# Attention into soft-MoE on one core: V products, transposes and batch work of a pair in one block on TensorE

## The chip, the cores and the metric

The kernel runs on one NeuronCore of a Trainium2 chip. Five engines work side by side, each with its own instruction queue in program order: TensorE (PE, matmuls; its weight loads are listed apart as PEld), VectorE (DVE), ScalarE (ACT), GpSimd (POOL) and SyncE (SP, used here only to issue transfers). Matrix products land in PSUM, which DVE and ACT read; transfers (DMAs) run between the chip's DRAM and SBUF on sixteen DMA engines. The metric is the device time of one execution in microseconds (us).

## The reference

Attention over 8 batches, 12 heads, 448 tokens and a head width of 64, whose denominator has one term more than a softmax, followed by a soft mixture of experts over the 3584 x 768 result. Cut to what matters:

```python
scores = q @ k.T / sqrt(64)
m = max(scores, axis=-1)
e = exp(scores - m)
attn = e / (sum(e) + exp(-m) + 1e-9)
x = (attn @ v)  as [8*448, 12*64]

logits = x @ phi                     # [3584, 32]: 8 experts, 4 slots each
d = softmax(logits, axis=0)          # over all 3584 tokens
slot_in = d.T @ x                    # [32, 768]
h = relu(slot_in[e] @ w1[e])         # 768 -> 1024, per expert
slot_out = h @ w2[e]                 # 1024 -> 768
c = softmax(logits, axis=1)          # over the 32 slots
out = c @ slot_out                   # [3584, 768]
```

## The kernel before

Heads are taken two at a time: 48 pairs, six to a batch, three to a "group" `g` that is loaded together. The two heads of a pair stand on partitions 0 to 63 and 64 to 127. Their score matmuls have 64 rows each, and neighbours in the queue that use different halves run at the same time; the V products and turns use all 128 rows. The schedule is manual: each engine runs its instructions in the order in which the Python code emits them, and semaphores follow from the tiles.

The parts of one pair `n`:

- `T(n)` transposes q and k by 28 small matmuls into one PSUM tile (`ps_t`, L224) and copies it to SBUF, on ACT for the first six pairs and the first pair of each group, else on DVE (L227, L229).
- `A`, `A1`: score blocks with queries on the partitions, for the row maxima. A pair has seven: six of 128x448 (L268 and L246) and one in which the two heads share a tile (L256). Each has its reduction on DVE into `mx` (L270, L250, L259).
- `W1(g)`, `W2(g)`, `W3(g)`, once for three pairs: POOL negates the maxima (L277), PE turns them into rows (L297, L298), ACT copies these to `mT` and takes the exponentials of the negated maxima, `ec` (L303, L306, L309).
- `Bk`, `AB`: score blocks with keys on the partitions (L354, L332), less the maximum by a second matmul that adds a row of `mT` (L358, L335), then ACT's exp into a buffer `e2` or `e1` (L360, L338). `AB` also emits `A1` blocks of a later pair, one ahead of its own matmuls and one behind.
- `V(g)` arranges v for a group, with a column of ones, on POOL.
- `AV(n, i, qs)`: V products, 32 matmuls of 65 columns per pair into `ps_av` (L393); the column of ones gives the sum of the exponentials.
- `N1(n)` copies `ps_av` to `ubuf` (ACT; DVE for the last four pairs; L405). `N2(n)` adds 1e-9 and `ec` to the sums and takes the reciprocal (two small DVE operations, L414, L415), then multiplies into `x` (three operations, L419, L423, L424, on POOL, for the last four pairs on DVE).
- `PX(n)` transposes the pair's part of x by four matmuls and ACT copies 512 columns to `xT` (L445, L451).

`P(b)` holds the mixture's work for one batch, as six steps: logits (L471) with their copy and row maxima; the turned logits (L496); the maximum over tokens (L508); the exponentials; the slot sums (L539) with the fading of what has been added so far; the turn of the combine weights (L544) and their sums `crec`.

The loop runs over `s` = 0 to 47, each with two half steps `y`, numbered `hs = 2s + y`. From hs = 5 on, the first half step emits two `AB` of pair s, then the last two i of the V products of pair s-1 for the three full query blocks, and its eight products for the fourth, then `N1`. The second emits one `AB`, `Bk(s, 3)` with the shared maxima block in it, `T(s+6)`, every third time W2 and W3, the first two i of the V products of pair s itself (12 matmuls), a step of P if one is due (`post`), `PX(s-2)`, and `N2(s-1)`. The maxima run four pairs ahead, so that none are left from s = 44 on. Loads by POOL follow at the end of each s: q and k, v, then expert weights, cast from f32 to bf16 on the way (`half_at`, `part_at`, `col_at`, `narrow_at`).

Buffers set the order as much as the queues do: PSUM pool `psA` has three banks, used in turn by the maxima blocks, `ps_t` and all tiles of P; `psB` has four, for the exp blocks, W2 and PX; `psV` one, for `ps_av`. There are five `e2` buffers and one `e1`.

The weights fill SBUF: eleven tiles `W` (w1 of eight experts, w2 of the first three), the twelfth half and the rest of w2 in `R`, where q, k, x and the exponentials lie, as these come free. The second column half of w2 for experts 4 to 7 is cast ahead into DRAM (`wd`) and brought in by SP (`load_second`, L141) at the end of attention.

Behind the loop stand the last batch's P, the hidden layers (`hidden`, L748: experts 0 to 3, then 4 to 7), the slot products (`slots`, L764), and the output, 3584 rows by 768 in f32, whose transfers fill the last 25 us.

Of the kernel before, what the change touches and what calls it, by code (L numbers as in the profile page):

```python
# [24 lines left out]
HG = 6  # L25
# [6 lines left out]
def kernel(  # L32
# [38 lines left out]
    ident2 = const.tile([128, 128], BF16, name="ident2")  # L71
# [7 lines left out]
    NQK, NE, VPN, NATV = 7, 5, HG * 4 * VS, HG * 4 * D  # L79
    sizes = [("nq0", 2 * NP * S), ("nq1", 2 * NP * S), ("nv", NATV), ("qk6", 2 * S), ("wm1", 512),  # L80
             ("qk0", 2 * S), ("qk1", 2 * S), ("qk2", 2 * S), ("wm0", 512), ("qk3", 2 * S), ("vp0", VPN),
             ("qk4", 2 * S), ("x0", 4 * DD), ("qk5", 2 * S), ("e2", NE * 2 * S), ("e1", S), ("vp1", VPN),
             ("xT", KC * 512), ("x1", 4 * DD)]
# [8 lines left out]
    e1_t = part("e1", 0, S)  # L92
# [3 lines left out]
    xT = part("xT", 0, KC * 512).rearrange("p (j s) -> p j s", j=KC)  # L96
# [23 lines left out]
    W = keep.tile([128, 11 * KC * F], BF16, name="W")  # L120
    w_tile = lambda i: W[:, i * KC * F:(i + 1) * KC * F]
# [10 lines left out]

    dram = ctx.enter_context(tc.tile_pool(name="dram", bufs=1, space=bass.MemoryType.DRAM))
    wd = [dram.tile([128, E2, ND], BF16, name=f"wd{z}") for z in range(FK)]

# [7 lines left out]
    with ExitStack() as at:  # L143
# [8 lines left out]
        ubuf = pu.tile([128, 2, 7 * W65], F32, name="ubuf")  # L152
# [27 lines left out]
        for h in range(2):  # L180
            nc.vector.tensor_add(ident2[:, 64 * h:64 * h + 64], ident[:, 0:64], ident[:, 64:128])
# [22 lines left out]
        mx, ngm, ec, mT, eT, av, us = {}, {}, {}, {}, {}, {}, {}  # L204
# [32 lines left out]
        def A(n, i):  # L237
# [4 lines left out]
            if i < 3:  # L242
# [5 lines left out]
                for hl in range(2):  # L248
                    c = HG * i + 2 * pl + hl
                    nc.vector.reduce_max(mx[g][:, c:c + 1], pss[hl][:, 0:S], axis=AX.X)  # L250
            else:
# [6 lines left out]
                c = 3 * HG + pl  # L258
                nc.vector.reduce_max(mx[g][:, c:c + 1], ps[:, 0:S], axis=AX.X)  # L259

        def A1(n, i, hl):
# [7 lines left out]
            c = HG * i + 2 * pl + hl  # L269
# [3 lines left out]
        def W1(g):  # L273
# [4 lines left out]
            cols = lambda t: t[:, 0:3 * HG].rearrange("p (i c) -> p i c", i=3)[:, :, 2 * l0:2 * l1]  # L278
            o = w[:, 0:3, :].rearrange("p i (d c) -> p i d c", d=2)[:, :, :, 2 * l0:2 * l1]
            neg(o, cols(m).unsqueeze(2).to_broadcast([128, 3, 2, 2 * (l1 - l0)]))  # L280
            for hl in range(2):
                r = slice(64 - 64 * hl, 128 - 64 * hl)
                o = w[r, 3, :].rearrange("p (d c) -> p d c", d=2)[:, :, 2 * l0 + hl:2 * l1:2]
                neg(o, m[r, 3 * HG + l0:3 * HG + l1].unsqueeze(1).to_broadcast([64, 2, l1 - l0]))
            if l1 - l0 == NP:
                neg(nm, m)
            else:
                nc.gpsimd.memset(nm, 0.0)
                neg(cols(nm), cols(m))
                neg(nm[:, 3 * HG + l0:3 * HG + l1], m[:, 3 * HG + l0:3 * HG + l1])  # L290
            ngm[g] = nm

        def W2(g):
# [4 lines left out]
            nc.tensor.matmul(ps[:, 384:448], w[:, 3, :], ident2[:, 0:64], start=True, stop=True)  # L298
            st["ps_m"] = ps

        def W3(g):
# [3 lines left out]
            e = psm.tile([128, NP, 7], F32, tag="ec", name="ec", bufs=3)  # L305
            nc.scalar.activation(e[:, :, 0:6].rearrange("p l (i h) -> p i l h", i=3),  # L306
                                 ngm[g][:, 0:18].rearrange("p (i l h) -> p i l h", i=3, h=2),
                                 AF.Exp, scale=scale)
            nc.scalar.activation(e[:, :, 6], ngm[g][:, 18:21], AF.Exp, scale=scale)  # L309
            ec[g] = e  # L310


        def Bk(n, i, c=0):
# [11 lines left out]
            else:  # L325
# [3 lines left out]
                es = [e1_t]  # L329
# [69 lines left out]
        def N1(n):  # L399
# [4 lines left out]
            u = ubuf[:, n % 2, :].rearrange("p (s c) -> p s c", c=W65)  # L404
# [3 lines left out]
        def N2(n):  # L408
            g, pl = divmod(n, NP)
            b, pb = divmod(n, PB)  # L410
            u = us[n]
            eng = nc.gpsimd if on_pool(n) else nc.vector
            rec = psm.tile([128, 7], F32, tag="rec", name="rec", bufs=3)
            nc.vector.scalar_tensor_tensor(rec, u[:, :, D], 1e-9, ec[mg(n)][:, pl, :], op0=ALU.add, op1=ALU.add)  # L414
            nc.vector.reciprocal(rec, rec)  # L415
            x = xb[b % 2]
            c = pb * 128
            rec2 = psm.tile([128, 2], F32, tag="rec2", name="rec2", bufs=3)
            eng.tensor_mul(  # L419
                x[:, 0:3, c:c + 128].rearrange("p i (h d) -> p i h d", h=2),  # L420
                u[:, 0:6, 0:D].rearrange("p (i h) d -> p i h d", h=2),
                rec[:, 0:6].rearrange("p (i h) -> p i h", h=2).unsqueeze(3).to_broadcast([128, 3, 2, D]))
            eng.tensor_scalar(rec2, halfm, rec[:, 6:7], None, op0=ALU.mult)  # L423
            eng.tensor_mul(  # L424
                x[:, 3, c:c + 128].rearrange("p (h d) -> p h d", h=2),
                u[:, 6, 0:D].unsqueeze(1).to_broadcast([128, 2, D]),
                rec2.unsqueeze(2).to_broadcast([128, 2, D]))
# [10 lines left out]
        def PX(n):  # L438
# [4 lines left out]
            for i in range(4):  # L443
                o = (i % 2 if two else i) * 128
                nc.tensor.matmul(pss[i // 2 if two else 0][:, o:o + 128], x[:, i, c], ident if i < 3 else ident2,  # L445
                                 start=True, stop=True)
            if two:
                nc.scalar.copy(xT[:, pb, 0:256], pss[0][:, 0:256])
                nc.vector.tensor_copy(xT[:, pb, 256:512], pss[1][:, 0:256])
            else:  # L450
                nc.scalar.copy(xT[:, pb, :], pss[0])  # L451
# [183 lines left out]
        for s in range(NPAIR):  # L635
            for y in range(2):
# [16 lines left out]
                if hs < 5:  # L653
                    T(hs + 3)
# [232 lines left out]
```

## Time and profile before

| | |
|---|---|
| median of three runs | 310.31 us (310.02 to 310.5) |
| the profiled execution | 310.7 us, span 308.9 us |
| busy shares of the span | PE 89%, DVE 83%, ACT 81%, POOL 66% |
| attention in its steady form | 40.5 to 242.9 us, s = 3 to 43 |
| last four pairs without maxima | 242.9 to 260.4 us |
| last batch, experts | 260.4 to 282.9 us |
| output | to 308.9 us |

The profile is one execution. A line of groups or of the timeline gives the engine, the kernel's line, the operation, the tile written and the tile read with shapes, and the count; in the timeline the first two numbers are the start and the length in us, and a bracket at the end tells the idle time of the engine before it and who ended it. Lengths of neighbours on one engine overlap, so the pace is read from starts. A line of stretches has the stretch, its length, the busy time and count of PE, PEld, DVE, ACT and POOL, the granted TensorE clock, the DMA share and GB/s.

### The profile page before, as it was taken

How to read it: one execution, taken by the hardware profiler on the slowest of the kernel's cores; microseconds unless marked ns; L12 is line 12 of the kernel's file. 1: busy time of each engine (PE TensorE's matmuls, PEld its weight loads, DVE VectorE, ACT ScalarE, POOL GpSimd, SP SyncE). 2: the span in 40 equal slices, each digit the busy share in tenths (PEclk: the TensorE clock that was granted, in tenths of full speed). 3: DMA queues.
4: the chain of work that ended last, by engine and by line, in shares of the span. 5: the costliest groups of instructions: out<-in, count | busy, mean ns of one | idle time of the engine just before them, and what ended most of it. 6: DMA issues, size and time to landing. Idle time of an engine off the chain costs nothing.

```text
span 308.9 us, 12205 instructions
## 1 busy us (share of the span) xinstructions
PE 275.6 (89%) x5067; PEld 159.0 (51%) x5068; DVE 257.2 (83%) x607; ACT 249.3 (81%) x549; POOL 202.7 (66%) x403
## 2 busy tenths in 40 slices
PE   2899999999999999999999999999999899994810
PEld 1434456565666656665566566656665556451200
DVE  4778999999999999999999999999999566536930
ACT  2357599999999999999999999999999997236810
POOL 8682769788788878896889788879584863000000
PEclk9999999999999999999999999999999999999555
DMA  6999499999999999999999999999971999937997
GB/s 88 149 128 202 64 205 150 198 182 205 163 196 157 210 169 198 155 203 149 149 164 186 177 186 169 196 177 203 166 110 17 144 126 204 337 128 260 415 439 312
DMA packets 49350, 57.44 MB, mean 186 GB/s; under 512 B 2832, under 2 KB 41488, under 8 KB 48912
## 3 DMA queue, kind: packets, MB, share of 16 engines
q0 software_dynamic: 45536, 42.52, 90.1%
q1 hardware_dynamic: 3760, 14.16, 11.5%
q8 instruction: 39, 0.64, 0.8%
q14 instruction: 15, 0.12, 0.1%
HBM read 88.18 MB, written 14.16 MB: 331 GB/s over the span
## 4 chain that ended last, share of the span: by engine, by line
PE 50%; DVE 30%; ACT 7%; issue 4%; POOL 4%; DMA 1%; DVEq 0%; POOLq 0%
DVE mx L270 15%; PE ps_av L393 11%; PE ps_a L268 6%; PE ps_t L224 6%; PE ps_b L354 5%; PE ps_b L358 4%; DVE mx L250 3%; DVE mx L259 3%; PE ps_b L332 3%; PE ps_a L246 2%; DVE W L801 2%; DVE R L229 2%; PE ps_x L445 2%; ACT R L227 2%; PE ps_so L764 2%
## 5 line engine op out<-in xcount | busy, mean ns | idle before, releaser
L270 DVE TENSOR_REDUCE mx<-ps_a 128x1 f32<-128x448 f32 x248 | 136.6, 613 | 5.3 <-PE ps_a L268 5.1
L360 ACT ACTIVATE R<-ps_b 128x448 bf16<-128x448 f32 x272 | 131.0, 573 | 1.1 <-PE ps_b L358 0.8
L268 PE MATMUL ps_a<-R 64*128 64x448 bf16 x248 | 80.5, 352 | 1.8 <-DVE mx L270 1.8
L354 PE MATMUL ps_b<-R 64*128 64x448 bf16 x272 | 73.9, 353 | 0.9
L358 PE MATMUL ps_b<-mT,sel 64*128 64x448 bf16 x272 | 70.6, 350 | 0.0
L393 PEld LDWEIGHTS <-R 128*128 128x128 bf16 (+1 forms) x1536 | 50.5, 101 | 30.5 <-issue 26.4
L393 PE MATMUL ps_av<-R 128*128 128x65 bf16 (+1 forms) x1536 | 64.9, 196 | 0.1
L419 POOL TENSOR_TENSOR R<-ubuf,rec 128x384 bf16<-128x384 f32 x44 | 36.3, 825 | 37.9 <-DVE rec L415 23.4
L224 PEld LDWEIGHTS <-R 64*64 64x64 bf16 x1344 | 31.1, 113 | 19.2 <-issue 7.8
L338 ACT ACTIVATE R<-ps_b 128x448 bf16<-128x448 f32 x64 | 36.0, 579 | 5.9 <-PE ps_b L335 5.9
L224 PE MATMUL ps_t<-ident,R 64*64 64x64 bf16 x1344 | 32.0, 198 | 5.9 <-DMA R<-in_q_dram 4.3
L451 ACT CAST R<-ps_x 128x512 bf16<-128x512 f32 x47 | 28.1, 598 | 5.7 <-PE ps_x L445 5.7
L259 DVE TENSOR_REDUCE mx<-ps_a 128x1 f32<-128x448 f32 x48 | 29.6, 616 | 0.6 <-PE ps_a L256 0.3
L358 PEld LDWEIGHTS <-sel 64*128 64x128 bf16 x272 | 21.5, 94 | 14.9 <-issue 5.3
L268 PEld LDWEIGHTS <-R 64*128 64x128 bf16 x248 | 23.1, 94 | 9.8
L405 ACT COPY ubuf<-ps_av 128x455 f32<-128x455 f32 x44 | 25.2, 573 | 3.0 <-PE ps_av L393 2.8
L227 ACT COPY R<-ps_t 128x896 bf16<-128x896 bf16 x20 | 18.4, 922 | 11.3 <-PE ps_t L224 11.0
L250 DVE TENSOR_REDUCE mx<-ps_a 128x1 f32<-128x448 f32 x40 | 22.6, 618 | 4.3 <-PE ps_a L246 3.9
L332 PE MATMUL ps_b<-R 64*64 64x448 bf16 (+1 forms) x112 | 22.7, 386 | 0.0
L335 PE MATMUL ps_b<-mT,sel 64*64 64x448 bf16 (+1 forms) x112 | 21.5, 366 | 0.0
L424 POOL TENSOR_TENSOR R<-ubuf,rec 128x128 bf16<-128x128 f32 x44 | 17.5, 398 | 3.7
L354 PEld LDWEIGHTS <-R 64*128 64x128 bf16 x272 | 17.2, 94 | 4.7 <-issue 0.2
(132 smaller groups left out, 454.0 us busy)
## 6 DMA issues: line engine op xcount, KB each, us to landing
W<-in_moe_w_dram POOLq DMA_DIRECT2D x22, 768.0 KB, 9.5
R<-in_v_dram POOLq DMA_DIRECT2D x32, 192.0 KB, 4.6
out_dram<-W SPq DMA_DIRECT2D x2, 2688.0 KB, 10.3
R<-in_q_dram POOLq DMA_DIRECT2D x15, 336.0 KB, 7.4
R<-in_k_dram POOLq DMA_DIRECT2D x15, 336.0 KB, 8.5
wd<-in_moe_w_dram POOLq DMA_DIRECT2D x8, 384.0 KB, 10.0
R<-wd SPq DMA_DIRECT2D x8, 384.0 KB, 8.6
R<-in_moe_w_dram POOLq DMA_DIRECT2D x2, 768.0 KB, 8.3
```

The lines of the kernel that those rows point to most:

```text
L224: nc.tensor.transpose(ps[r, a, c:c + 64], src[r, pl, tok * D:(tok + 1) * D], ident[r, r])
L250: nc.vector.reduce_max(mx[g][:, c:c + 1], pss[hl][:, 0:S], axis=AX.X)
L259: nc.vector.reduce_max(mx[g][:, c:c + 1], ps[:, 0:S], axis=AX.X)
L268: nc.tensor.matmul(ps[:, 0:S], t[r, 0, i * 128:(i + 1) * 128], t[r, 1, :], start=True, stop=True)
L270: nc.vector.reduce_max(mx[g][:, c:c + 1], ps[:, 0:S], axis=AX.X)
L332: nc.tensor.matmul(outs[hl], t[rs[hl], 1, cols], t[rs[hl], 0, :], start=True, stop=False)
L338: nc.scalar.activation(e, p[:, 0:S], AF.Exp, scale=scale)
L354: nc.tensor.matmul(ps[hl][:, 0:S], t[rs[hl], 1, cols], t[rs[hl], 0, :], start=True, stop=False)
L358: nc.tensor.matmul(ps[hl][:, 0:S], sel[rs[hl], h:h + 1].to_broadcast([64, 128]), mT[mg(n)][rs[hl], :], start=False, stop=True)
L360: nc.scalar.activation(e[:, hl, :], ps[hl][:, 0:S], AF.Exp, scale=scale)
L393: nc.tensor.matmul(o, eT[n, i, hl][:, qc], vp[g % 2][:, 2 * pl + hl, i, 0:W65], start=(i == 0 and u == 0 and hl == 0), stop=(i == 3), skip ...
L419: eng.tensor_mul(x[:, 0:3, c:c + 128].rearrange("p i (h d) -> p i h d", h=2), u[:, 0:6, 0:D].rearrange("p (i h) d -> p i h d", h=2), rec[: ...
```

## The change

1. **One block a pair.** In steps before the last four, the first half step has no V products. The second emits, behind its `AB`, `Bk`, `T` and W2/W3: the step of P if one is due, `PX(s-4)` for `PX(s-2)`, all 32 V products of pair s-1, and `N1(s-1)`. P's steps start at hs = 2(6b+10)+1, one per second half step, so always in the block; those of batch 5 are drawn together, and batch 6 has hs = 90 to 94 where it had 87 to 91. For the V products a step later there are six `e2` and two `e1`. In the last four steps the order is about that of before, with PX of pairs 40 to 45 at set places (`px_at`).
2. **Denominators of two pairs.** `N2` takes two pairs at once: the two DVE operations on 128x14, and five POOL operations. It stands in the first half step of every odd s, behind the two `AB`. For it `ubuf` has four buffers, the maxima are stored pair by pair, and the exponentials stand in one ring `ecr` of six pairs, written by one ACT operation in W3 instead of two.
3. **Transposed x of 448 columns** instead of 512. The logits of the last 64 tokens of a batch are computed by two matmuls into the two halves of their tile, 30 matmuls instead of 24. `ident2` is 64 wide.
4. **crec** gets its 1e-9 and reciprocal once at the end for all batches.
5. **More weights via DRAM.** `W` is half a tile shorter. The second half of the rows of w2 of expert 2 is cast into DRAM (`w2d`, at s = 36) and brought by SP into the place of w1 of expert 3 behind `hidden(0)`; the first column half of expert 7 goes through `w3d` (at s = 37) and is brought by SP ahead of the wd loads. In the last batch the turned logits come ahead of the plain ones.

```diff
-    W = keep.tile([128, 11 * KC * F], BF16, name="W")
+    NW = 21 * KC * F // 2
+    W = keep.tile([128, NW], BF16, name="W")
...
+    w_two = W[:, 3 * KC * F:3 * KC * F + FH * DD]
+
+    def w2_at(e, c, kt):
+        if e == 2 and kt >= FH:
+            return w_two[:, (kt - FH) * DD + c * ND:(kt - FH) * DD + (c + 1) * ND]
+        return w_col[e][c][:, kt, :]
...
+    def narrow_first():
+        gdma(out=w3d, in_=moe_w2[E - 1, :, 0:ND].rearrange("(j p) f -> p j f", p=128))
+
+    def narrow_two():
+        src = moe_w2[2, FH * 128:FK * 128, :]
+        gdma(out=w2d.rearrange("p (j f) -> p j f", f=DD), in_=src.rearrange("(j p) f -> p j f", p=128))
...
-        ubuf = pu.tile([128, 2, 7 * W65], F32, name="ubuf")
+        ubuf = pu.tile([128, 4, 7 * W65], F32, name="ubuf")
...
-        def N2(n):
...
+        def N2(*ns):
+            k, n0 = len(ns), ns[0]
...
+            rec = psm.tile([128, 14], F32, tag="rec", name="rec", bufs=2)[:, 0:7 * k]
...
+            nc.vector.scalar_tensor_tensor(rec, den, 1e-9, ecr[:, 7 * (n0 % 6):7 * (n0 % 6 + k)], op0=ALU.add, op1=ALU.add)
             nc.vector.reciprocal(rec, rec)
...
-                nc.scalar.copy(xT[:, pb, :], pss[0])
+                nc.scalar.copy(xT[:, pb, :], pss[0][:, 0:S])
...
-                    for i in range(4):
+                    for i in range(3):
                         nc.tensor.matmul(v["ps_l"][:, i, :], xT[:, j, i * 128:(i + 1) * 128], phi_sb[:, j, :],
                                          start=(j == 0 and i == 0), stop=(j == KC - 1), skip_group_check=True)
+                for j in js:
+                    for r in (slice(0, 64), slice(64, 128)):
+                        nc.tensor.matmul(v["ps_l"][r, 3, :], xT[:, j, 384:S], phi_sb[:, j, :],
+                                         start=False, stop=(j == KC - 1), skip_group_check=True)
...
-                nc.vector.tensor_scalar(r, r, 1e-9, None, op0=ALU.add)
-                nc.vector.reciprocal(r, r)
...
-                post[2 * (PB * b + PB + 2) + z + (z > 2) + (z > 4) if b < B - 2 else 2 * (PB * b + PB + 2) - 1 + z] = f
+                hs = 2 * (PB * b + PB + 4) + 1
+                post[hs + 2 * z - (max(z - 2, 0) if b == B - 3 else 0) if b < B - 2 else hs - 3 + z] = f
...
+        px_at = {88: (40,), 89: (41,), 92: (42,), 93: (43, 44), 95: (45,)}
...
+                tail = s >= NPAIR - 4
                 if y == 0:
-                    if 0 <= s - 1:
+                    if tail:
                         for i in (2, 3):
                             AV(s - 1, i, range(3))
+                    elif s % 2 and s >= 3:
+                        N2(s - 3, s - 2)
...
-                    if s < NPAIR:
+                    if tail:
                         for i in (0, 1):
                             AV(s, i, range(3))
-                if 2 * s + y in post:
-                    post[2 * s + y]()
+                if hs in post:
+                    post[hs]()
...
-                if y and 0 <= s - 2 < NPAIR - 2 and s - 2 != n6:
-                    PX(s - 2)
...
+                if y and not tail:
+                    if s < NPAIR - 5 and s >= 4:
+                        PX(s - 4)
+                    if s:
+                        for i in range(4):
+                            AV(s - 1, i, range(3))
                         for i in range(4):
                             AV(s - 1, i, [3])
                         N1(s - 1)
...
-                load_half(half_at[s - 2], 1)
+                if half_at[s - 2] < 10:
+                    load_half(half_at[s - 2], 1)
+                else:
+                    narrow_two()
+            if s == 37:
+                narrow_first()
...
+        nc.sync.dma_start(out=late[0][:, 3, :, :], in_=w3d)
         load_second(0, 4)
...
         hidden(0, h0, range(2))
+        nc.sync.dma_start(out=w_two, in_=w2d)
         last[3]()
+        nc.vector.tensor_scalar(crec, crec, 1e-9, None, op0=ALU.add)
+        nc.vector.reciprocal(crec, crec)
```

## The prediction

> **What bounds the kernel now.** I read the page first: the busy shares, then the chain of waits.
>
> ```profile
> span 308.9 us, 12205 instructions
> PE 275.6 (89%) x5067; PEld 159.0 (51%) x5068; DVE 257.2 (83%) x607; ACT 249.3 (81%) x549; POOL 202.7 (66%) x403
> DVE mx L270 15%; PE ps_av L393 11%; PE ps_a L268 6%; PE ps_t L224 6%; PE ps_b L354 5%; PE ps_b L358 4%; DVE mx L250 3%; DVE mx L259 3%; PE ps_b L332 3%; PE ps_a L246 2%; DVE W L801 2%; DVE R L229 2%; PE ps_x L445 2%; ACT R L227 2%; PE ps_so L764 2%
> L270 DVE TENSOR_REDUCE mx<-ps_a 128x1 f32<-128x448 f32 x248 | 136.6, 613 | 5.3 <-PE ps_a L268 5.1
> ```
>
> The chain alternates between VectorE's row maxima and TensorE. Next the busy time by stretches: from 40.5 to 242.9 us lie the 41 steps s=3 to 43, 4.94 us each.
>
> ```profile
> 40.50:242.90 202.40, 198.83 (x3960) 122.53 (x3958) 192.76 (x454) 193.58 (x442) 164.46 (x321) 1.00 1.08 171
> 242.90:260.40 17.50, 16.64 (x271) 9.24 (x268) 9.97 (x36) 16.33 (x39) 11.33 (x23) 1.00 1.01 144
> ```
>
> PE, DVE and ACT (first, third and fourth pair of numbers) are all above 95% there; in the last steps DVE falls off and ACT rules. Shares can't separate three such engines, so I went to the timeline of single steps.
>
> ```profile
> 148.83 0.36 PE L268 MATMUL ps_a<-R 64*128 64x448 bf16 x1
> 149.22 3.38 DVE L270 TENSOR_REDUCE mx<-ps_a 128x1 f32<-128x448 f32 x6 [0.34 <-PE ps_a L268]
> 150.34 0.78 PE L393 MATMUL ps_av<-R 128*128 128x65 bf16 x20
> 151.05 0.36 PE L268 MATMUL ps_a<-R 64*128 64x448 bf16 x1
> 152.13 0.63 PE L224 MATMUL ps_t<-ident,R 64*64 64x64 bf16 x28
> 152.69 0.54 PE L393 MATMUL ps_av<-R 128*128 128x65 bf16 x12
> 153.06 0.39 PE L445 MATMUL ps_x<-ident,R 128*128 128x128 bf16 x4
> 153.38 0.36 PE L268 MATMUL ps_a<-R 64*128 64x448 bf16 x1
> 153.59 0.16 DVE L414 SCALAR_TENSOR_TENSOR rec<-ubuf,ec 128x7 f32<-128x7 f32 x1
> 153.89 2.18 DVE L270 TENSOR_REDUCE mx<-ps_a 128x1 f32<-128x448 f32 x4
> 154.53 0.35 PE L268 MATMUL ps_a<-R 64*128 64x448 bf16 x1
> ```
>
> A step without batch work lasts 4.55 us (148.83 to 153.38). Call its seven score blocks for the maxima A1 to A7 and their reduces r1 to r7. psA has three buffers, shared with the transposes T, and PE issues in program order; so A4 waits for r1, A7 for r4 and T for r5. That shows at 153.89: r1 starts, and A4 starts 0.64 later. The other steps of the loop, from starts: A1 to r1 0.39; reduce to reduce 0.535 (six in 3.20 from 139.52 to 142.72); T to what follows 0.56; V products 0.031 each (12 in 0.37), and 0.09 more for the way back to 64-row matmuls (20 in 0.71); PX with that way back 0.32; the two small operations of N2 0.30 (153.59 to 153.89). The loop before is then: r1 at 0.51 (N2's pair stands ahead of it), T at 0.51 + 4 x 0.535 + 0.64 = 3.29, then 0.56 + 0.37 + 0.32: 4.54, against 4.55 measured. The block of 20 V products costs nothing in it: it lies between A4 and A5 while DVE works off r2 to r4.
>
> **The change, part by part.**
>
> *One block.* The 20 V products of the first half step move behind T, PX and the other 12. The half steps then join: A1 to A7 come with nothing between and each waits for a reduce. r1 starts at 0.39, T at 0.39 + 2.14 + 0.64 = 3.17. Behind T: 0.56, PX 4 x 0.057 less its 64 columns = 0.20, 32 x 0.031 + 0.09 = 1.08. Next A1 at 5.01, next r1 at 5.40. DVE then has r6, r7 and at best T's copy in stock, 3 x 0.535 from 3.07, and stands empty from 4.67 to 5.40. Before, the same way (0.56 + 0.37 + 0.32 + 0.39 = 1.64) was covered by 1.60 and N2's 0.30; where ACT copies T, the cover is 0.53 shorter and the trace shows the idle 0.34 at 149.22. So the step goes from 4.55 to 5.01. One mode switch less per pair (0.09) is in this.
>
> *Denominators of two pairs.* Half as many small operations, 20 pairs of them less (0.30 each, 6 us of DVE). But they move from the end of a step to behind r4 of every odd one, ahead of r5, for which T waits. There they cost 0.30 in each of about 20 odd steps: +6.0; nothing is the other end, if they fell into an idle place. I take 6.0, since r5's block is ready long before r4 ends. The 128x14 form isn't in the trace; 128x7 takes 0.16 and 0.20, 128x32 operands 0.19 (L511), so I leave 0.30. On POOL three operations per pair (0.83, 0.29, 0.40) become five per two pairs, some 2.8 in one go, and stand ahead of the step's loads, V copies and W1, which gets one more operation of 0.3; POOL is 81% busy, loads are issued two groups ahead, and PX comes at least 1.5 steps (7 us) behind N2: 0. If POOL fell behind, PX and W2 would wait on PE's queue, with all V products behind them.
>
> *Batch work.* All steps of P now stand in the block, where DVE is starved, so their PE time adds: logits 30 matmuls for 24 (0.61 becomes 0.76), turned logits 0.14, maxima 0.15, slot sums 0.69, combine turn 0.06: 1.80 for each of six batches = 10.8. W2 adds 0.21 thirteen times = 2.7. The removed pair on crec (0.17 + 0.18) saved DVE time that is now idle anyway: 0; at the end one pair of 128x32 stands where two stood.
>
> *Sum, steps 3 to 43.* 41 x 5.01 = 205.4; + 6.0 + 10.8 + 2.7; steps 42 and 43 have no T, so no wait for r5: -1.4; 12 more V products in step 43: +0.4; no PX in step 3: -0.2. Together 223.7. The same book for before (41 x 4.55 + 2.7 + 9.9 + 1.8 on crec) gives 201.0 against 202.4 measured. The difference is 21.3 by the measured and 22.7 by the booked value: **+22.0**.
>
> *Last four steps.* ACT is the bound (16.33 of 17.5 busy). PX of pairs 40 and 41 falls into them: 2 x 0.44, less 0.06 for each of six narrower copies: **+0.5**. The narrower copies and the one exp fewer in W3 elsewhere save ACT time that isn't the bound: 0. P(6) comes three half steps later, and its sums are due only by the last batch's: 0.
>
> *Weights via DRAM.* Half of w2 of expert 2 comes back by SP behind the first hidden stage, which ends at 268.65 (L748), and its rows are needed at 273.15 (half through the slot products, from 272.51). A 768 KB output transfer took 4.3 us uncontended: landing at 273.0; the eight loads from wd, 384 KB, took 5.9 to 11.0 while queues were full. The queues are busy to about 272.6 (406 GB/s at 270 to 272, 140 after); 0.79 MB behind them takes 1.9: 274.5, 1.4 late, and TensorE waits with all that follows: **+1.4**, ends 0 and 6.6. The first column half of expert 7 replaces casting loads of the same size and is due at 274.2, after an issue near 259: 0. On SP it stands ahead of the wd loads and delays them by the 1.9 us of its bytes; these are due at 279.0, in the last slot products, and there were 6 us to spare: 0. POOL issues as many DMAs as before (two to DRAM and one split load for three). By the Trainium skill ("DMA: Bandwidth & Descriptors", section "Anatomy of one DMA") a transfer takes some 2.0 us and its bytes at 436 GB/s, an estimated 3.8 us here; the load would be there at 272.6 and the 1.4 would go; the rows of the contended loads speak against it.
>
> Before step 3 the same V products only change place: 0, give or take 1. Sum: 22.0 + 0.5 + 1.4 = +23.9. The profiled execution took 310.7 (span 308.9), 0.4 over the median 310.31; on the median this gives **334.2**.
>
> **Rivals.**
>
> *PE's saving decides: faster.* DVE's sum falls by 20 pairs x 0.30 and 6 x 0.30, and if its idle time stayed as it is, six steps would shrink from 29.87 (199.29 to 229.16, like reduces of two batches) by 6 x 0.15 + 0.30 = 1.2: 41/6 x 1.2 = -8.2; with the end's +1.9: 304. For it speaks PE's 98%, the highest share. It holds if the next r1 comes within 1.6 us of r5's end; the rows make it 2.3. The Trainium skill ("Perfetto Trace Analysis", section "Matmul Optimizations") says the same way that matmuls should go back to back in batches since the engine's power follows its use; the granted clock of 1.00 in the whole stretch leaves that nothing to win here. 0.09.
>
> *Half the bubble.* A7, let in by r4, starts at 0.39 + 3 x 0.535 + 0.64 = 2.63, the last matmuls of its half step 0.21 later (L335) and T could follow 0.19 after these: 3.03. Were r5 done by then, 0.14 x 39 = 5.5 would go; and N2's pair may fall into a gap: -6.0. 334.2 - 11.5 = 322.7. 0.15.
>
> *The late weights.* The load takes the 11.0 us of the slowest wd load: lands at 279.75, 6.6 late: 339.4. 0.06.
>
> Forecast 0.69; no difference (within 0.2%, about what this kernel's runs can tell apart), when the rival gain and the end's losses cancel: 0.01.
>
> **Numbers.** The low end takes all lower bounds: N2 -6.0, no wait for r5 -5.5, V products without the switch -3.1, weights -1.4: 318; I set 317. High: late weights +5.2, V products at 0.0355 (20 in 0.71) +2.5, the start +1: 343. Left out is mainly the faster rival, and a little on each side. Faster 0.09, same 0.01, slower 0.90.
>
> **What would show it.** Right: DVE reduces with idle times of 0.6 to 1.2 us behind PE once a step; PE waiting for the reduce of L270 in nearly every step, where it waited six times; DVE near 82% and ACT near 85% in the long stretch (their work less what is saved, over 224 us); the step 5.0 even, 5.3 odd. The chain would go r1 to r5, T, V products. Wrong: DVE still above 95% busy, then the rival holds. A wait of slot products for a DMA shows the weights. The weakest places are the additive batch work and whether r5 really gates T in each step.

## The result and the profile after

| | before | after |
|---|---|---|
| median of the compared runs | 310.16 us (309.75 to 310.50, 4 runs) | 340.09 us (337.86 to 342.12, 4 runs) |
| profiled execution, and its span | 310.7, 308.9 us | 341.48, 339.7 us |

The changed kernel takes 1.0964 times as long, 95% interval 1.0881 to 1.1047: 29.9 us more by the medians, where 23.9 were forecast and the range ended at 343.

The page of the changed kernel: the span, the busy shares, the chain of waits by line, and the group of row maxima (its last figures are the idle time of VectorE ahead of these reduces, and what ended most of it).

```profile
span 339.7 us, 12348 instructions
PE 286.3 (84%) x5115; PEld 165.0 (49%) x5116; DVE 249.8 (74%) x548; ACT 250.0 (74%) x532; POOL 193.8 (57%) x394
DVE mx L289 31%; PE ps_av L405 14%; PE ps_t L243 9%; PE ps_a L287 5%; DVE mx L269 4%; PE ps_x L463 3%; DMA W<-w2d 2%; PE ps_o L835 2%; PE ps_a L265 2%; PE ps_b L366 2%; PE ps_so L803 2%; PE ps_s L562 1%; DVE rec L429 1%; PE ps_l L489 1%; DVE W L843 1%
L289 DVE TENSOR_REDUCE mx<-ps_a 128x1 f32<-128x448 f32 x248 | 136.2, 611 | 38.7 <-PE ps_a L287 25.0
```

L289, L287, L243 and L405 are the reduces, the score blocks of the maxima, T and the V products (L270, L268, L224 and L393 before). The reduces themselves cost what they cost before (136.2 against 136.6 us). What grew is the idle time ahead of them, from 5.3 to 38.7 us, and their share of the chain, from 15% to 31%. No engine is above 84% busy over the span.

The stretches, with the columns as before. The first line is steps s=3 to 43, the second from step 44 to the first hidden stage.

```profile
40.34:269.51 229.17, 207.61 (x3984) 127.25 (x3979) 186.38 (x399) 194.44 (x425) 156.98 (x315) 0.99 0.97 150
269.51:294.55 25.04, 23.26 (x400) 14.13 (x398) 12.61 (x46) 18.50 (x45) 10.54 (x23) 1.00 0.92 181
```

DVE and ACT fill 81% and 85% of the long stretch (186.38 and 194.44 of 229.17), where both were above 95%. Cut at the same instructions in both traces, the span divides so:

| section | before | after | difference | forecast |
|---|---|---|---|---|
| up to step 3 | 40.50 | 40.34 | -0.2 | 0 |
| steps 3 to 43 | 202.42 | 229.17 | +26.75 | +22.0 |
| step 44 to the first hidden stage | 22.96 | 25.04 | +2.1 | +0.5 |
| first hidden stage | 6.56 | 6.57 | 0 | 0 |
| first slot products, up to the next turn | 1.42 | 2.50 | +1.1 | +1.4 |
| from there to the end | 35.04 | 36.08 | +1.0 | 0 |

Two steps in the timeline of the changed kernel: an even one from 189.23 (its first score block lies above the cut) and an odd one from 194.33.

```profile
190.84 0.35 PE L287 MATMUL ps_a<-R 64*128 64x448 bf16 x1 [0.18 <-DVE mx L289]
192.43 0.63 PE L243 MATMUL ps_t<-ident,R 64*64 64x64 bf16 x28
192.99 0.23 PE L531 MATMUL ps_bc<-ident,sm 128*128 128x128 bf16 x1
193.06 0.36 PE L463 MATMUL ps_x<-ident,R 128*128 128x128 bf16 x4
193.25 1.14 PE L405 MATMUL ps_av<-R 128*128 128x65 bf16 x32
194.33 0.36 PE L287 MATMUL ps_a<-R 64*128 64x448 bf16 x1
194.72 2.22 DVE L289 TENSOR_REDUCE mx<-ps_a 128x1 f32<-128x448 f32 x4 [0.86 <-PE ps_a L287]
196.86 0.17 DVE L428 SCALAR_TENSOR_TENSOR rec<-ubuf,ecr 128x14 f32<-128x14 f32 x1
197.06 0.24 DVE L429 RECIPROCAL rec<-rec 128x14 f32<-128x14 f32 x1
197.22 1.09 DVE L289 TENSOR_REDUCE mx<-ps_a 128x1 f32<-128x448 f32 x2
197.83 0.63 PE L243 MATMUL ps_t<-ident,R 64*64 64x64 bf16 x28 [0.46 <-DVE mx L289]
198.60 1.14 PE L405 MATMUL ps_av<-R 128*128 128x65 bf16 x32
199.67 0.36 PE L287 MATMUL ps_a<-R 64*128 64x448 bf16 x1
200.14 2.22 DVE L289 TENSOR_REDUCE mx<-ps_a 128x1 f32<-128x448 f32 x4 [0.77 <-PE ps_a L287]
```

T, a small matmul of the batch work (L531), PX and 32 V products follow each other on PE (192.43 to 194.33), VectorE runs out of score blocks meanwhile and stands empty for 0.86 us until A1 of the next step is there, and for 0.77 us behind the odd step. The two idle times aren't of one kind: T of the step from 189.23 is copied by ACT, and VectorE has two small operations of the batch in that place; T of the next one VectorE copies itself. In the odd step N2's two operations (196.86, 197.06) stand between r4 and r5, and T waits 0.46 for r5. T starts 3.20 us behind the even step's start and 3.50 behind the odd one's; the book had 3.17 and 3.47.

### The profile page after: what moved, and what is told of

It reads as the page before. It is cut to its first block, busy times and chain, and to the rows that moved or that the text cites. A ratio compares the mean times of both kernels' runs of the same rounds, so it can differ in the third digit from the quotient of the medians.

```text
span 339.7 us, 12348 instructions
## 1 busy us (share of the span) xinstructions
PE 286.3 (84%) x5115; PEld 165.0 (49%) x5116; DVE 249.8 (74%) x548; ACT 250.0 (74%) x532; POOL 193.8 (57%) x394
## 4 chain that ended last, share of the span: by engine, by line
PE 47%; DVE 40%; issue 3%; DMA 3%; ACT 3%; DVEq 0%; POOL 0%; ACTq 0%; POOLq 0%
DVE mx L289 31%; PE ps_av L405 14%; PE ps_t L243 9%; PE ps_a L287 5%; DVE mx L269 4%; PE ps_x L463 3%; DMA W<-w2d 2%; PE ps_o L835 2%; PE ps_a L265 2%; PE ps_b L366 2%; PE ps_so L803 2%; PE ps_s L562 1%; DVE rec L429 1%; PE ps_l L489 1%; DVE W L843 1%
## 5 line engine op out<-in xcount | busy, mean ns | idle before, releaser
L289 DVE TENSOR_REDUCE mx<-ps_a 128x1 f32<-128x448 f32 x248 | 136.2, 611 | 38.7 <-PE ps_a L287 25.0
L372 ACT ACTIVATE R<-ps_b 128x448 bf16<-128x448 f32 x272 | 124.6, 562 | 4.6 <-PE ps_b L370 4.4
L287 PE MATMUL ps_a<-R 64*128 64x448 bf16 x248 | 80.6, 353 | 7.6 <-DVE mx L289 7.4
L370 PE MATMUL ps_b<-mT,sel 64*128 64x448 bf16 x272 | 71.6, 352 | 0.1
L435 POOL TENSOR_TENSOR R<-ubuf,rec 128x384 bf16<-128x384 f32 x44 | 36.4, 826 | 43.5 <-DVE rec L429 23.9
L405 PE MATMUL ps_av<-R 128*128 128x65 bf16 (+1 forms) x1536 | 56.3, 195 | 2.2 <-issue 1.7
L405 PEld LDWEIGHTS <-R 128*128 128x128 bf16 (+1 forms) x1536 | 48.6, 100 | 7.7 <-issue 4.8
L243 PEld LDWEIGHTS <-R 64*64 64x64 bf16 x1344 | 31.3, 114 | 31.4 <-issue 26.5
L243 PE MATMUL ps_t<-ident,R 64*64 64x64 bf16 x1344 | 32.1, 198 | 16.9 <-DVE mx L289 8.6
L350 ACT ACTIVATE R<-ps_b 128x448 bf16<-128x448 f32 x64 | 35.6, 574 | 6.0 <-PE ps_b L347 6.0
L417 ACT COPY ubuf<-ps_av 128x455 f32<-128x455 f32 x44 | 23.7, 539 | 14.9 <-PE ps_av L405 14.1
L287 PEld LDWEIGHTS <-R 64*128 64x128 bf16 x248 | 23.3, 94 | 15.5 <-issue 10.0
L370 PEld LDWEIGHTS <-sel 64*128 64x128 bf16 x272 | 24.8, 95 | 12.2 <-issue 2.5
L469 ACT CAST R<-ps_x 128x448 bf16<-128x448 f32 x47 | 25.2, 540 | 4.4 <-PE ps_x L463 4.2
L296 POOL TENSOR_SCALAR R<-mx 128x18 bf16<-128x18 f32 (+5 forms) x68 | 16.8, 253 | 10.3 <-DVE mx L269 6.3
L347 PE MATMUL ps_b<-mT,sel 64*64 64x448 bf16 (+1 forms) x112 | 22.4, 387 | 0.1
```

Source lines behind the costliest of these rows:

```text
L243: nc.tensor.transpose(ps[r, a, c:c + 64], src[r, pl, tok * D:(tok + 1) * D], ident[r, r])
L287: nc.tensor.matmul(ps[:, 0:S], t[r, 0, i * 128:(i + 1) * 128], t[r, 1, :], start=True, stop=True)
L350: nc.scalar.activation(e, p[:, 0:S], AF.Exp, scale=scale)
L370: nc.tensor.matmul(ps[hl][:, 0:S], sel[rs[hl], h:h + 1].to_broadcast([64, 128]), mT[mg(n)][rs[hl], :], start=False, stop=True)
L372: nc.scalar.activation(e[:, hl, :], ps[hl][:, 0:S], AF.Exp, scale=scale)
L405: nc.tensor.matmul(o, eT[n, i, hl][:, qc], vp[g % 2][:, 2 * pl + hl, i, 0:W65], start=(i == 0 and u == 0 and hl == 0), stop=(i == 3), skip ...
```

## Experiments

Each kernel is compared with runs of the kernel before that were timed beside it: 311.31 us (7 runs) beside those with 12 and 20 products moved, with late N2 and with four psA buffers; 311.37 us (11 runs) beside the one with batch work first and the one with two pairs in before's order; 311.12 us (23 runs) beside the other four. Ratios are to these, with 95% intervals. The 340.09 us of the changed kernel were timed beside 310.16, so differences of medians to it are uncertain by about 1 us. The theory: the block starves VectorE, N2's place ahead of r5 adds to it, and batch work in the starved place costs its PE time.

### 12 of the 32 V products back in the first half step

```diff
                     elif s % 2 and s >= 3:
                         N2(s - 3, s - 2)
+                    if s and not tail:
+                        for i in (0, 1):
+                            AV(s - 1, i, range(3))
...
                     if s:
-                        for i in range(4):
+                        for i in (2, 3):
                             AV(s - 1, i, range(3))
```

> The changed kernel with 12 of the 32 V products of pair s-1 (its first two i) moved back into the first half step, behind the two AB; the other 20 stay in the block. Theory of the starved reduces: the 12 hide behind r2 to r4, T stays gated by r5, so each step's block is 12 x 0.031 = 0.37 shorter over some 39 steps: -14.5, to 325.6 from 340.1. Rival, PE's own work decides: the products cost the same wherever they stand and there is one more mode switch of 0.09 per step: about 343.

Measured: 325.36 us (323.77 to 326.85), ratio 1.0478 [1.0428, 1.0528], 0.2 off what the theory said (325.6). Nothing else of the change was touched, and half of the loss to before is gone. The rival's 343 falls.

### 20 of them, as before the change

```diff
+                    if s and not tail:
+                        for i in (0, 1):
+                            AV(s - 1, i, range(3))
+                        for i in range(4):
+                            AV(s - 1, i, [3])
...
                     if s:
-                        for i in range(4):
+                        for i in (2, 3):
                             AV(s - 1, i, range(3))
-                        for i in range(4):
-                            AV(s - 1, i, [3])
```

> The same with 20 of the 32 in the first half step (the first two i and the eight of the fourth query block). Starved reduces: the block is 0.62 shorter, the loop would be 4.39, DVE's own reduces, copies and small operations then need 4.43, so -0.58 in 39 steps: -22.6, to 317.5; N2's 0.30 in odd steps stays. Every step further than 12 products saves less than 0.031 a product. PE's own work decides: about 343 again.

Measured: 318.6 us (317.42 to 320.25), ratio 1.0248 [1.0194, 1.0303], 1.1 above what the theory said (317.5); span 315.6. The window of steps 3 to 43 of this kernel, and its group of reduces:

```profile
40.65:244.49 203.84, 198.16 (x3981) 124.76 (x3979) 187.00 (x400) 189.82 (x427) 156.79 (x314) 1.00 1.07 169
L289 DVE TENSOR_REDUCE mx<-ps_a 128x1 f32<-128x448 f32 x248 | 136.2, 610 | 12.7 <-PE ps_a L287 8.2
```

The long stretch is 203.84 us, 1.4 more than before the change, against 229.17 with the block. So taking 20 products out of the block gives back 25.3 of the 26.75 us; 2.2 of these are a pause of PE, told of in the last section, that the changed kernel's profile has and this one lacks. PE's work is the same in both (3981 and 3984 matmuls). The idle time of the reduces fell from 38.7 to 12.7 us. What is left of this kernel's loss, 5.1 of its 6.7 us of span, lies behind the long stretch.

### All 32, and N1, in the first half step

```diff
+                    if s and not tail:
+                        for i in range(4):
+                            AV(s - 1, i, range(3))
+                        for i in range(4):
+                            AV(s - 1, i, [3])
+                        N1(s - 1)
...
-                    if s:
-                        for i in range(4):
-                            AV(s - 1, i, range(3))
-                        for i in range(4):
-                            AV(s - 1, i, [3])
-                        N1(s - 1)
```

> The changed kernel with all 32 V products of pair s-1 and N1 behind the two AB of the first half step; the block behind T keeps PX and the batch work. Starved reduces: the products are now longer than r2 to r4 hide, T starts at 3.48 instead of 3.17 and the loop is 4.33, while DVE needs 4.43 as with 20: no further gain, 318.6 give or take 2. Rival, each product taken out of the block saves its 0.031 whatever stands around it (the first two points, 1.23 and 0.85 us a product over the kernel, read as a line): 12 x 0.85 = -10, to 308.

Measured: 315.95 us (314.62 to 318.01), ratio 1.015 [1.0084, 1.0216]. That is 0.65 below the theory's 316.6 to 320.6 and far from the rival's 308. The first 12 products moved gave 14.7 us, the next 8 gave 6.8, the last 12 gave 2.65. These 2.65 don't come from the loop: steps 3 to 43 take 204.74 us here and 203.84 with 20 products, but step 3 starts 2.35 us earlier (at 38.30 for 40.65), which isn't explained. The gain per product falls as the hole behind T closes, and past 20 products the loop gains nothing, as the theory said. The chain of waits of this kernel shows what took over: PE with 66%, DVE with 12%.

```profile
PE 66%; DVE 12%; ACT 8%; issue 3%; DMA 3%; POOL 3%; DVEq 0%; POOLq 0%; ACTq 0%
PE ps_av L405 15%; PE ps_a L287 9%; PE ps_b L366 8%; PE ps_b L370 7%; PE ps_t L243 6%; DVE mx L269 5%; PE ps_b L344 4%; DVE mx L289 3%; PE ps_x L463 3%; ACT R L246 3%; ACT R L469 2%; PE ps_o L835 2%; DMA W<-w2d 2%; PE ps_b L347 2%; PE ps_so L803 2%
```

The reduces' share of the chain went from 31% to 3%.

### N2 of two pairs behind T instead of ahead of r5

The operations, their number and their shapes are the same; the ring of exponentials is twice as long, since they are read later.

```diff
-        ecr = psm.tile([128, 6 * 7], F32, name="ecr", bufs=1)
+        ecr = psm.tile([128, 12 * 7], F32, name="ecr", bufs=1)
...
-                    elif s % 2 and s >= 3:
-                        N2(s - 3, s - 2)
...
                         T(s + 6)
+                    if s % 2 and s >= 3 and not tail:
+                        N2(s - 3, s - 2)
```

> The changed kernel with N2 of two pairs moved from behind the two AB of an odd step to behind T of the same step (the ring of exponentials is twice as long so that W3 need not wait). If N2's two operations on DVE delay r5 and with it T: 0.30 in each of some 20 odd steps goes, -6.0, to 334.1, and odd and even steps last alike. Rival: they fell into idle time already, or whatever they free is taken up by the wait for the next reduce: 340.1.

Measured: 332.38 us (331.78 to 335.12), ratio 1.0705 [1.0646, 1.0764]. The timeline of this kernel in an odd step, and its row of T's waits (total, times, longest) from 40 to 265 us:

```profile
152.75 0.17 DVE L428 SCALAR_TENSOR_TENSOR rec<-ubuf,ecr 128x14 f32<-128x14 f32 x1
153.87 2.21 DVE L289 TENSOR_REDUCE mx<-ps_a 128x1 f32<-128x448 f32 x4 [0.53 <-PE ps_b L366]
```

```profile
PE ps_t L243 <- DVE mx L289: 0.5, 3, 0.2
```

The same row of the changed kernel:

```profile
PE ps_t L243 <- DVE mx L289: 8.6, 19, 0.5
```

N2 now falls into VectorE's hole, T's wait is gone, and odd steps with little or no batch work last 5.03 to 5.09 us, as the even ones do. The place of two small operations cost 7.7 us by the medians.

### Four buffers for psA, three for psB

```diff
-        psA = pool("psA", 3, space=PSUM)
-        psB = pool("psB", 4, space=PSUM)
+        psA = pool("psA", 4, space=PSUM)
+        psB = pool("psB", 3, space=PSUM)
```

> The changed kernel with four banks for psA and three for psB (four and four before), nothing else. Starved reduces: A5 to A7 and T wait for one reduce earlier, T for r4, so T starts 0.535 earlier: 4.47 instead of 5.01 in each of 39 steps, -21, to 319. If the third psB bank was needed, ACT's exps come later and part of it is lost, at most all. Rival, PE's own work: no gain, 340 or more.

Measured: 331.06 us (330.09 to 334.99), ratio 1.0669 [1.0592, 1.0746]: a miss. T waits for no reduce any more, but the steps shrank only by what N2's place cost (odd and even 5.06; steps 3 to 43 take 220.92 us, 220.72 with late N2). The medians show more because step 3 starts 4.5 us earlier (35.87 for 40.34), of which the last four steps lose 1.8 again. The row that shows why is one of the waits from 45 to 235 us:

```profile
PE ps_b L366 <- ACT R L372: 21.7, 70, 0.6
```

The scores of the exponentials now wait for ACT to free one of three psB buffers, and ACT's share of the chain is 33%, where it was 3%. The wait moved from one ring to the other, and with the bound on T alone gone the hole behind T stays.

### The kernel before with the same buffers

The same two lines in the kernel before the change.

> The kernel before with four banks for psA and three for psB, nothing else. Starved reduces: before, DVE was in stock through the block, so the fourth psA bank gives nothing, while scores now wait for the exp three before them, as in the changed kernel with these banks (5.06 a step): slower, 320 to 330. Rival, the fourth bank helps any order: faster than 311.

Measured: 316.05 us (315.58 to 316.75), ratio 1.0139 [1.009, 1.0189]: slower as expected, by less than the 320 to 330 named. In before's order the exchange of a buffer costs some 5 us: 7.7 in steps 3 to 43 (210.11 for 202.42) and 1.8 in the last four, while step 3 starts 4.0 us earlier (36.54 for 40.50). Its chain of waits names ACT's exponentials:

```profile
PE 51%; ACT 28%; DVE 8%; issue 4%; POOL 4%; DVEq 0%; POOLq 0%; ACTq 0%
```

### Batch work in the first half step

```diff
-                hs = 2 * (PB * b + PB + 4) + 1
-                post[hs + 2 * z - (max(z - 2, 0) if b == B - 3 else 0) if b < B - 2 else hs - 3 + z] = f
+                hs = 2 * (PB * b + PB + 4)
+                post[hs + 2 * z - (max(z - 2, 0) if b == B - 3 else 0) if b < B - 2 else hs - 2 + z] = f
```

> The changed kernel with the steps of P one half step earlier, in the first half step behind the two AB instead of in the block (batch 6 stays). Starved reduces: PE's 1.80 a batch leaves the block and hides behind r2 to r5, but P's operations on DVE (copies, maxima, fading and adding, some 2.3 a batch), which stood in the idle place, now stand between r4 and r5, for which T waits: +0.5 a batch, about 343. Rival, the batch work's PE time simply adds wherever it stands: 340. If PE's time went and DVE's cost nothing: -10.8, 329.

Measured: 340.75 us (339.73 to 341.9), ratio 1.0945 [1.09, 1.099]. The medians lie between the two theories and don't tell them apart. The steps do: of five rounds of six steps four last 33.91 to 34.21 us, against 33.47 in the changed kernel (the first one 33.19), so most batches cost some 0.5 more there, as expected. The P steps weren't too dear for their place; they lose as much or more in the other one. Their tiles there take psA buffers that a reduce has to free; for the turned logits the wait is (whole run):

```profile
PEld ps_lT L519 <- DVE mx L289: 4.8, 6, 0.8
```

### 20 V products first, and N2 late

Both edits of above together.

> 20 V products in the first half step and N2 behind T, both changes together. With the bubble gone DVE has work in stock through the block, so N2's 0.30 is on its path wherever it stands, except where ACT copies T (a third of the steps): starved reduces expects -2 from the 318.6 of 20 products alone, 316.5. Rival, the gain of the later N2 (-7.7 alone) adds: 311.

Measured: 313.14 us (311.69 to 315.52, 9 runs), ratio 1.0057 [1.002, 1.0093]. The profiled execution, a tenth, took 317.94 us and is left out; its rows aren't compared. The median lies between the two theories: late N2 gives 5.5 us on top of the 20 products, 7.7 without them. With both undone the change is still no gain; in the kernel with the 20 products alone 5.1 us of loss lay behind step 43, and nothing here touches that part.

### Before's order with the denominators of two pairs

N2 of two pairs for pairs 0 to 35, in before's place behind `AV(..., [3])`, one exponential, 448-wide transposed x, crec at the end; V products, batch work and weights as before.

```diff
-                    if 0 <= s - 1 and on_pool(s - 1):
+                    if 36 <= s - 1 and on_pool(s - 1):
                         N2(s - 1)
+                    if 2 <= s <= 36 and s % 2 == 0:
+                        N2(s - 2, s - 1)
...
+                if y == 0 and s % 2 and 0 <= s - 3 < 36:
+                    PX(s - 3)
```

> The order of the kernel before, with the parts of the change that save work: N2 of two pairs at once for pairs 0 to 35 (behind the second one's half step, PX of the even pair a half step later), maxima stored by pairs and one exp in W3, 448 columns of transposed x, crec once at the end. Weights, exp buffers, V products and batch work as before; ubuf keeps two buffers. If reduces and small operations of DVE bound the steps whose T DVE copies: 0.15 a pair in two thirds of 36 pairs = -3.6, and -1.8 for crec: 305.7. Rival: with two ubuf buffers ACT's copy of the next V products waits for POOL's multiplies of two pairs (2.8 in one go), and V products with it: the gain goes, 310 or more.

Measured: 314.51 us (312.79 to 315.1, 6 runs), ratio 1.0094 [1.0063, 1.0125]. It is slower, as the rival said, but by another way than it named: N1 never waits for POOL. POOL itself stands ready for N2's reciprocals (waits of the whole run), and PX waits a little for POOL's multiplications (its weight loads 3.7 us in 13 times):

```profile
POOL R L416 <- DVE rec L410: 39.7, 20, 4.6
```

Steps 3 to 43 take 205.85 us (202.42 before), and the end 36.64 (35.04 before). Half as many small operations on VectorE thus bought nothing in sum. The steps differ: of steps 28 to 33 the even ones take 4.92, 4.23 and 5.28 us (5.16, 4.98, 5.41 before), the odd ones, each with PX of two pairs, 5.67, 4.74 and 5.31 (4.88, 4.56, 4.88 before). Which of the parts makes the 3.4 us isn't settled; 1.1 of it are two pauses of PE of the kind told of in the last section.

### The kernel before with crec finished once

```diff
                 nc.vector.reduce_sum(r, v["cd"][:, 0:4, :], axis=AX.X)
-                nc.vector.tensor_scalar(r, r, 1e-9, None, op0=ALU.add)
-                nc.vector.reciprocal(r, r)
...
         last[3]()
+        nc.vector.tensor_scalar(crec, crec, 1e-9, None, op0=ALU.add)
+        nc.vector.reciprocal(crec, crec)
```

> The kernel before with one part of the change alone: 1e-9 and reciprocal of crec once at the end for all batches (two operations of 0.17 and 0.18 less in each of seven batches, two at the end). Where DVE is the bound, in steps whose T it copies, 0.30 a batch goes: -1.8, to 309.5, if each of the seven falls into such a step; nothing if PE's batch work decides those steps.

Measured: 309.45 us (307.71 to 312.0, 12 runs), ratio 0.9942 [0.9908, 0.9975]. This one small part of the change, alone, makes the kernel before 0.6% faster, and the interval lies below 1. Steps 3 to 43 take 202.07 us, only 0.35 less than before, where the book had put 1.8 on crec. Single steps show the saving: the two operations stood at the start of steps 12, 18, 24, 30, 36 and 42, ahead of r1, and steps 18, 24 and 36 take 4.58, 4.59 and 4.59 us (4.98, 4.99 and 4.98 before), 0.40 less for the 0.35 that the two cost. In steps 12, 30 and 38 PE pauses by 0.90, 0.53 and 0.30 us (the last section tells for what), which takes most of it back in this one execution. In a stretch where VectorE is 95% busy and stands on the chain, its small operations count. In the changed kernel the sums of crec (L570) end 4.83 us behind a step's start, in VectorE's hole, so the saving can't be worth the same there; no run tested that.

## Why the prediction was right, and which terms were off

**The mechanism** is shown. Taking 20 products out of the block gives back 25.3 of 26.75 us in the long stretch with no other edit (23.1 of 24.6 without the pause). The announced signs are there: reduces idle 0.69 to 1.23 us once a step (steps 3 to 42, but 2.67 in step 39, behind the pause), where before they were idle in 13 steps, by 0.30 to 0.57; DVE 81% and ACT 85%; the chain through L289, T and L405. The idle was named as 4.67 to 5.40 after a step's start (0.73) where VectorE copies T; the row of that kind above has 0.77.

**The step without batch work** was booked at 5.01 even and 5.31 odd and took 5.04 and 5.34 (even ones with the small matmul L531 5.09). One point stays finer than the trace: that r5 gates T in *every* step. T stands at the booked time in both kinds of step, but only the 19 odd ones show an idle PE ahead of it; in the even ones PE's own work ends at that same time. What PE waits for in nearly every step is a reduce that lets in a score block of the maxima (whole run):

```profile
PE ps_a L287 <- DVE mx L289: 7.4, 40, 0.2
```

**Batch work is additive**, called a weak place, held: a round of six steps was booked at 33.2 us and took 33.47 (5.88, 5.76, 5.09, 5.34, 6.01, 5.39), 29.87 before.

**N2 ahead of r5** was booked at 6.0 and measured by its removal at 7.7 (medians). In the long stretch the removal is 8.5 (229.17 to 220.72), which holds the 2.2 of the pause below; 6.2 without it.

**Steps 3 to 43: +22.0 booked, +26.75 measured.** The book's total was 223.7. Of the 5.5 above it, step 38 holds 2.2: it took 7.88 us where the like steps take 6.0, and step 39 took 5.69 for 5.40. The book had no such term: PE stops in the midst of the V products (timeline of the changed kernel; the count is that of the products on either side), for its own instructions, as the last section shows:

```profile
238.21 0.74 PE L405 MATMUL ps_av<-R 128*128 128x65 bf16 x19
240.65 0.56 PE L405 MATMUL ps_av<-R 128*128 128x65 bf16 x13 [1.71 <-issue]
```

Another 1.1 is step 43 (6.51 us): its slot sums wait 0.52 for r5 and its V products 0.33 for psV, which has one buffer. The remaining 2.2 are 0.05 a step.

**The last four steps: +0.5 booked, +2.1 measured.** This is the term that the prediction mis-sized most in proportion. It is the same 25.04 in the kernels with 12 and 20 products moved, with N2 late and with batch work earlier, and 22.99 in before's order with two-pair N2 and 448-wide x, where PX and P have before's places. So neither the V products and N2 of the earlier steps nor the width make it. That leaves the new order of the end, and with it what else that last kernel has as before: N2 of the pairs 42 and 43 one by one, five `e2`, and the weights. By steps, 44 is 0.3 us shorter than before, 45 and 46 are 0.6 and 0.3 longer and 47 is 1.5 longer; what follows up to the first hidden stage takes the same. Where the 1.5 come from, the trace of the changed kernel only suggests:

```profile
283.24 1.03 ACT L469 CAST R<-ps_x 128x448 bf16<-128x448 f32 x2
285.16 0.75 PE L562 MATMUL ps_s<-cd,R 128*128 128x32 bf16 x24
286.91 0.98 ACT L372 ACTIVATE R<-ps_b 128x448 bf16<-128x448 f32 x2 [0.88 <-PE ps_b L370]
```

Two copies of PX stand on ACT, the slot sums of batch 6 then stand between V products on PE, and ACT waits 0.88 for its scores; step 47 takes 5.2 us (3.8 before). The prediction had ACT's two copies, but took P(6), three half steps later, for free. No run undid PX or P(6) alone, so the cause stays argued.

**Weights via DRAM: +1.4 booked, +1.1 measured**, and by the wait that was named:

```profile
302.86 0.32 PE L803 MATMUL ps_so<-W 128*32 128x384 bf16 x1 [0.75 <-DMA W<-w2d]
296.72 0.32 SPq L811 DMA_DIRECT2D W<-w2d  x1
```

Issued at 296.72, the rows let PE go at 302.86, 6.1 us later. The queues were full meanwhile: they moved 295 to 409 GB/s from 296.7 to 301, and the last of the wd loads landed at 300.98. The estimate of 3.8 us by the Trainium skill ("DMA: Bandwidth & Descriptors", section "Anatomy of one DMA") would have made no wait; the trace doesn't agree. The fit in that section is for transfers issued from GpSimd, and this one is issued by SP while others run. In the other kernels with this load whose rows are compared the section is 2.2 to 3.6 us long, so the wait's size is not steady, and that 1.1 came out near 1.4 is partly luck.

**The end: 0 booked, +1.0 measured**, and not explained. From the second turn of slot products on the instructions are the same. The sixth output transfer is issued 10.79 us behind that turn in both kernels and lands 15.90 us behind it, 14.41 before; the later ones stay behind, too. Kernels with all weight changes have 35.8 to 36.3 us there, before's order with four psA buffers or with crec at the end 34.8 and 35.1; but the two-pair kernel, which has no weight change, has 36.64. So the weights are not shown to be its cause.

**Rivals.** "PE's saving decides" fell: with VectorE's work lowered (187.00 us busy in the long stretch with 20 products moved, 192.76 before), that stretch stayed above before's 202.42 in every kernel with the two-pair N2 whose rows are compared (203.84 to 229.17). "Half the bubble" put T at 3.03; it stands at 3.20.

**Of the experiments**, the four-buffer psA was forecast wrong (319 for 331.06): its doubt that psB needs its fourth bank was the answer, and should have been priced first, on the chain rather than in words. The two-pair kernel in before's order was, too (305.7 for 314.51), and before's order with four psA buffers lay below its range (320 to 330 for 316.05).

## What to carry to other kernels

Work of PE that fills a time in which it must wait for another engine anyway is free there; gathered into one block behind the operation that is let in last, it starved the engine that was the bound, and cost more than the gathering saved. Before moving work, write the loop down as a recurrence (who lets in which block, with the ring's buffers) from starts in the timeline: here it gave 33.2 us for a round of 33.47, where three engines above 95% busy told nothing. The Trainium skill ("Perfetto Trace Analysis", section "Optimization Strategy") reads a gap that repeats on the engine that should be saturated as a possible want of buffers; here one more buffer, taken from another ring, mostly moved the wait (331.06 of 340.09 us, with 21.7 us of new waits), and the order of the work was the larger part (315.95).

## What was not expected of the hardware

PE paused for 1.71 us in the midst of a run of products, though no row names a wait, and behind the pause the granted clock fell. What PE waited for can be told from the trace: its own instructions. They are brought in by transfers, in packets of 16 KB (queue, kind: packets, MB, share of 16 engines):

```profile
q8 instruction: 40, 0.66, 0.7%
```

PE's instructions number 10240 in this trace (5115 matmuls, 5116 weight loads and 9 of its sequencer), 256 for each packet. In the order of their starts 7873 of them stand ahead of the pause, which is 30 x 256 + 193. The 30th packet landed at 239.10, and PE went on at 240.65, 1.55 us later. The twelve profiles of this case have 17 pauses of 0.15 us or more ahead of a matmul of PE for which no wait is named. Each stands at place 193 of such a count by 256 and ends 1.33 to 1.57 us behind the landing of the last packet; and in all twelve the number of packets landed at each place 193 is the number of whole 256s before it. Besides this one and one of 1.75 us (in the profile of 20 products with late N2 that is left out above) the longest is 0.90 us; the kernel before has none. Why a packet comes late isn't shown, nor whether the runs without a profile had such pauses.

The windows of the changed kernel (the number behind the five engines is the clock):

```profile
239.00:240.00 1.00, 0.00 (x0) 0.00 (x0) 0.00 (x0) 0.00 (x0) 0.00 (x0) 1.00 1.21 183
242.00:243.00 1.00, 1.00 (x8) 0.53 (x6) 1.00 (x3) 0.99 (x3) 0.00 (x0) 0.50 1.31 205
```

All engines stand still from 239 to 240; the clock is 0.50 from 242 to 245 and back at 1.00 from 246. So a pause under 2 us and what followed cost some 2.2 us in all. The Trainium skill ("TensorE: Matmul & The Clock Gate", section "What's actually happening") lets the clock fall after an idle window of about 3.4 us; here it fell after half of that. Behind the pause of 1.75 us it stayed at 1.00, so such a pause alone doesn't decide it.

The other surprise is the weight of place. Two operations of VectorE, 0.17 and 0.24 us long and run in every second step, cost 7.7 us of 340 where r5 waits behind them, and nothing that can be seen behind T in the same step.
